# Retention by running state in 36 software-pipelined steps of 128 tokens, in place of full score blocks with the second layer behind

## The chip, the cores and the metric

The kernel runs on one core of one Trainium2 chip. The metric is device microseconds of one execution. Before the change the median of six executions is 512.67 us (512.37 to 516.56).

## The reference

Two layers: multi-head retention (attention with a causal, exponentially decaying mask and no softmax), then a feed-forward layer with a SoLU activation and a layer norm.

```python
# q, k, v: [8 batches, 8 heads, 576 tokens, 64]
scores = (q @ k.T) / sqrt(64)
ret    = scores * where(i >= j, gamma[h] ** (i - j), 0)   # gamma[h] = 1 - 2**(-5-h)
x      = (ret @ v)                                        # as [4608 tokens, 512]
h      = x @ w_in                                         # [4608, 1024]
solu   = h * exp(h - max(h)) / sum(exp(h - max(h)))
ln     = (solu - mean(solu)) / sqrt(var(solu) + 1e-6) * g_ln
out    = ln @ w_out                                       # [4608, 512]
```

## The kernel before

**First layer.** `attention_pair` handles one batch and two heads; it is called 32 times (8 batches, 4 pairs). It loads q, k and v of the pair by twelve DMAs on SP's queue, scales q by gamma^p and k by gamma^-p (p is the token's place in its block of 128) on ScalarE while casting to 16 bits, transposes them on TensorE (L264) and evacuates the transposes (L269 on VectorE, L270 on ScalarE). For each head, all causal score blocks are formed by matmuls with the 64 rows of the head (L283, up to 448 columns at a time), multiplied on VectorE by a table of decays `Gd_sb` that also holds the causal mask (L290), and multiplied by v in two accumulations avA and avB of 288 tokens (L306), whose stationary operand is 64 columns wide. The results go to `xT`, which holds the transposed x of all 4608 tokens (L315, L319).

**Second layer.** The 36 tiles of 128 tokens are handled in groups of four or five. `moe_tile_p1` does h (L131, eight 512-column matmuls), exp with the row sum (L138), the product (L144), mean and variance (L148, L151). After a group's last tile `moe_rstd` takes one square root on ScalarE for the group. `moe_tile_p3` subtracts the mean (L175), transposes on TensorE (L185), evacuates (L188), does the second product (L191, eight 512-column matmuls), scales by 1/std while evacuating (L198) and sends 256 KB out from GpSimd's queue (L201).

**What sets the order.** A scheduler of the framework orders the instructions within each engine by priority and data; the source gives the steps of the batch before after each pair (the loop at L339 to L353). So on TensorE matmuls of the two layers stand between one another. Weights are loaded and cast at the start (L77 to L98), ahead of the first q, k and v on the same queue.

Of the kernel before, what the change touches and what calls it, by code (L numbers as in the profile page):

```python
# [10 lines left out]
F16 = mybir.dt.float16  # L12


def _np_tables():
    H = 8
    P = 128
    gammas = 1.0 - 2.0 ** (-5.0 - np.arange(H, dtype=np.float64))
    p = np.arange(P)
    gq = (gammas[None, :] ** p[:, None]) / 8.0  # L20
    gk = gammas[None, :] ** (-p[:, None])
    rel = p[None, :] - p[:, None]
    M = 576
# [18 lines left out]
def kernel(  # L42
# [14 lines left out]
    P = 128  # L57
    NC = 5
# [3 lines left out]
    gq_np, gk_np, Gd_np, id_np, gammas = _np_tables()  # L62

    const_pool = ctx.enter_context(tc.tile_pool(name="const", bufs=1))
    big_pool = ctx.enter_context(tc.tile_pool(name="big", bufs=1))

    ident = const_pool.tile([P, P], F16)
    gq_sb = const_pool.tile([P, H], FP)
    gk_sb = const_pool.tile([P, H], FP)
    Gd_sb = const_pool.tile([P, H, 576], FP)  # L70
    nc.sync.dma_start(out=ident, in_=nc.inline_tensor(id_np, name="ident").ap())
    nc.sync.dma_start(out=gq_sb, in_=nc.inline_tensor(gq_np, name="gq").ap())
    nc.sync.dma_start(out=gk_sb, in_=nc.inline_tensor(gk_np, name="gk").ap())
# [46 lines left out]
    def moe_tile_p1(t, gi):  # L120
# [26 lines left out]
        for half in range(2):  # L147
# [240 lines left out]
```

## Time and profile before

| | before |
|---|---|
| median of six executions | 512.67 us |
| the profiled execution | 512.37 us |
| its span, first to last instruction | 510.6 us |
| TensorE (PE) busy | 419.2 us, 82% |
| VectorE (DVE) busy | 336.5 us, 66% |
| ScalarE (ACT) busy | 256.9 us, 50% |
| GpSimd (POOL) busy | 19.8 us, 4% |
| mean granted clock of TensorE | 0.877 |
| moved by DMA | 44.8 MB |

The busy share of an engine counts the time in which at least one of its instructions is under way, so a matmul at the lower of the two clocks counts twice as long as at the higher, and a busy TensorE need not be one that does much. "Pitch" below is the time from the start of one matmul to the start of the next. Where a row of the timeline merges n instructions, the pitch is the row's length less one single duration, divided by n - 1.

### The profile page before, as it was taken

Reading aid. Unit: us, or ns where it says so; the run is one execution under the profiler, and the core shown is the slowest. Engines: PE = TensorE matmul, PEld = TensorE weight load, DVE = VectorE, ACT = ScalarE, POOL = GpSimd, SP = SyncE. Lnnn points to the kernel's source line nnn. Section 1 sums busy time; section 2 is a strip of 40 time slices with the busy share of each in tenths; the row PEclk is TensorE's granted clock in tenths of the full one; section 3 lists DMA queues with packets and bytes.
Section 4 is the critical chain, followed back from the end, with each engine's and each line's share of the span. In section 5 each row is a group of like instructions: output and inputs, shape, how many; then the busy total and the mean of one; then the engine's idle time right before and its main releaser. Section 6 shows DMA issues by size and latency. Waiting matters only on the chain.

```text
span 510.6 us, 6542 instructions
## 1 busy us (share of the span) xinstructions
PE 419.2 (82%) x2080; PEld 184.1 (36%) x2080; DVE 336.5 (66%) x953; ACT 256.9 (50%) x597; POOL 19.8 (4%) x40
## 2 busy tenths in 40 slices
PE   0088998989979898889969898889969899789774
PEld 0033443334523443344423444333423444244341
DVE  0256667684788658684588658784687758784850
ACT  1343446445854558154844569144844468043642
POOL 0000000000000100000000010000000000000001
PEclk9999999559978899599978899598987899699979
DMA  7855531426450345214440345204440241000002
GB/s 294 276 121 127 117 89 29 92 66 152 127 112 2 89 127 119 48 35 113 119 98 1 86 113 126 59 24 112 123 104 1 68 116 37 1 22 34 29 22 83
DMA packets 122835, 44.79 MB, mean 88 GB/s; under 512 B 118832, under 2 KB 118832, under 8 KB 122672
## 3 DMA queue, kind: packets, MB, share of 16 engines
q1 hardware_dynamic: 119920, 34.94, 28.2%
q0 software_dynamic: 2880, 9.44, 4.9%
q8 instruction: 16, 0.26, 0.2%
q14 instruction: 19, 0.16, 0.1%
HBM read 34.91 MB, written 9.44 MB: 87 GB/s over the span
## 4 chain that ended last, share of the span: by engine, by line
PE 64%; DVE 19%; ACT 9%; DMA 4%; issue 3%; SPq 1%; POOL 0%; POOLq 0%; ACTq 0%; DVEq 0%
PE ops L191 15%; PE qk L283 15%; PE avB L306 11%; PE hps L131 7%; PE avA L306 6%; DVE stats L148 6%; DVE solu_g L144 6%; DMA gln_sb<-in_moe_g_ln_dram 4%; PE lntp L185 3%; DVE retT L290 3%; PE tk L264 3%; ACT lnT_sb L188 3%; PE tq L264 3%; ACT khT L270 1%; DVE ln_sb L175 1%
## 5 line engine op out<-in xcount | busy, mean ns | idle before, releaser
L290 DVE TENSOR_TENSOR retT<-qk,Gd_sb 128x288 f16<-128x288 f32 (+4 forms) x384 | 150.2, 428 | 81.3 <-PE qk L283 80.4
L283 PE MATMUL qk<-qhT,khT 64*128 64x288 f16 (+4 forms) x384 | 113.0, 326 | 28.6 <-DVE solu_g L144 12.1
L191 PE MATMUL ops<-w2p_sb,lnT_sb 128*128 128x512 f16 x288 | 88.3, 430 | 7.5 <-ACT lnT_sb L188 5.7
L306 PE MATMUL avB<-retT,v 128*64 128x288 f16 (+2 forms) x320 | 93.5, 320 | 0.0
L131 PE MATMUL hps<-w_in_sb,xT 128*128 128x512 f16 x288 | 84.2, 426 | 7.3 <-DVE solu_g L144 7.3
L306 PEld LDWEIGHTS <-v 128*64 128x64 f16 (+1 forms) x512 | 51.5, 122 | 76.4 <-issue 55.5
L138 ACT ACTIVATE e_sb<-hps 128x512 f32<-128x512 f32 x72 | 42.8, 596 | 49.8 <-PE hps L131 34.7
L283 PEld LDWEIGHTS <-khT 64*128 64x128 f16 (+1 forms) x384 | 34.3, 101 | 78.1 <-issue 54.1
L306 PE MATMUL avA<-retT,v 128*64 128x288 f16 (+2 forms) x192 | 54.6, 288 | 0.1
L144 DVE TENSOR_TENSOR solu_g<-hps,e_sb 128x512 f32<-128x512 f32 x72 | 48.7, 683 | 8.9 <-ACT e_sb L138 8.8
L188 ACT COPY lnT_sb<-lntp 128x1024 f16<-128x1024 f16 x36 | 36.0, 1013 | 25.2 <-PE lntp L185 24.8
L198 ACT ACTIVATE out_sb<-ops,rstd_g 128x512 f32<-128x512 f32 x36 | 24.6, 684 | 47.6 <-PE ops L191 29.6
L148 DVE BATCH_NORM_STATS2 stats<-solu_g 128x6 f32<-128x512 f32 x72 | 46.2, 679 | 0.1
L131 PEld LDWEIGHTS <-xT 128*128 128x128 f16 x288 | 28.3, 104 | 45.9 <-issue 22.8
L264 PE MATMUL tq<-ident,q 128*128 128x128 f16 (+1 forms) x160 | 21.8, 234 | 27.5 <-ACT q L238 27.2
L191 PEld LDWEIGHTS <-lnT_sb 128*128 128x128 f16 x288 | 27.5, 106 | 45.8 <-issue 18.4
L315 ACT CAST xT<-avA 64x288 f16<-64x288 f32 x32 | 12.5, 391 | 61.7 <-PE avA L306 61.4
L201 POOL DMA_DIRECT2D out_dram<-out_sb x36 | 19.6, 543 | 486.5 <-ACT out_sb L198 468.8
L185 PE MATMUL lntp<-ident,ln_sb 128*128 128x128 f16 x288 | 28.6, 240 | 11.8 <-DVE ln_sb L175 11.8
L175 DVE TENSOR_SCALAR ln_sb<-solu_g,mu_g 128x512 f16<-128x512 f32 x72 | 31.2, 479 | 3.8 <-PE lntp L185 3.6
L246 ACT ACTIVATE k<-k_sb,gk_sb 128x256 f16<-128x256 f32 x64 | 32.2, 503 | 0.0
L238 ACT ACTIVATE q<-q_sb,gq_sb 128x256 f16<-128x256 f32 x64 | 32.1, 502 | 0.0
(32 smaller groups left out, 275.7 us busy)
## 6 DMA issues: line engine op xcount, KB each, us to landing
out_dram<-out_sb POOLq DMA_DIRECT2D x36, 256.0 KB, 2.6
q_sb<-in_q_dram SPq DMA_DIRECT2D x64, 128.0 KB, 2.4
k_sb<-in_k_dram SPq DMA_DIRECT2D x64, 128.0 KB, 2.4
v_sb<-in_v_dram SPq DMA_DIRECT2D x64, 128.0 KB, 2.4
Gd_sb<-Gd SPq DMA_DIRECT2D x1, 2304.0 KB, 9.1
w_in_f<-in_moe_w_in_dram SPq DMA_DIRECT2D x1, 2048.0 KB, 13.7
w_f<-in_moe_w_out_dram SPq DMA_DIRECT2D x1, 2048.0 KB, 19.0
q_sb<-in_q_dram SPq DMA_DIRECT2D x64, 16.0 KB, 2.4
```

The costliest lines, as they stand in the source:

```text
L131: nc.tensor.matmul(out=ps, lhsT=xT[:, dc, tok0 : tok0 + P], rhs=w_in_sb[:, dc, hh], start=(dc == 0), stop=(dc == 3),)
L138: nc.scalar.activation(out=e_sb[:, hh], in_=ps, func=ACT.Exp, accum_out=sums[:, half : half + 1],)
L144: nc.vector.tensor_tensor(out=solu_g[:, gi, hh], in0=ps, in1=e_sb[:, hh], op=ALU.mult)
L148: nc.vector.bn_stats(out=stats[:, half], in_=solu_g[:, gi, half * 512 : (half + 1) * 512])
L175: nc.vector.tensor_scalar(out=ln_sb[:, hh], in0=solu_g[:, gi, hh], scalar1=mu_g[:, gi : gi + 1], scalar2=None, op0=ALU.subtract, op1=ALU.b ...
L185: nc.tensor.transpose(out=tps[:, c], in_=ln_sb[:, c * P : (c + 1) * P], identity=ident)
L188: nc.scalar.copy(out=lnT_sb, in_=tps)
L191: nc.tensor.matmul(out=o_ps, lhsT=lnT_sb[:, c], rhs=w2p_sb[:, c], start=(c == 0), stop=(c == 7),)
L264: nc.tensor.transpose(out=dst_ps[:, c * P : c * P + ncol], in_=src[rows, c, :], identity=ident[rows, rows],)
L283: nc.tensor.matmul(out=ps[0:jsz, 0:pw], lhsT=khT[dd, j0 : j0 + jsz], rhs=qhT[dd, i0:i1], start=True, stop=True,)
L290: nc.vector.tensor_tensor(out=retT[jb][0:jsz, i0:i1], in0=ps[0:jsz, 0:pw], in1=Gd_sb[0:jsz, h, i0 - j0 : i1 - j0], op=ALU.mult,)
L306: nc.tensor.matmul(out=av[:, lo - i0 : i1 - i0], lhsT=v16[0:jsz, jb, dd], rhs=retT[jb][0:jsz, lo:i1], start=(n == 0), stop=(n == len(jbs) ...
```

## The change

The kernel function is written anew; inputs, outputs and the arithmetic of the reference stay.

- **Retention by state.** Only the diagonal 128x128 score block of each chunk is formed. What earlier chunks give is carried in a state per head, the decayed sum of k-transposed times v (64x64), kept in `gt`: `kv_mm` forms a chunk's part, `state` adds it and decays it by gamma^128 (`g128`).
- **Steps.** The work is cut into 36 steps of 128 tokens with all eight heads: four whole chunks of each batch, and one step for the two 64-token remainders of two batches together. Each step goes through both layers. `x` of a step lives in a small tile, not in a buffer of all tokens.
- **Who does what.** Scaling and casting q, k, v, and the decay and cast of the state, go to GpSimd, as do three operations on one element per partition, the last of them the power -1/2 (so there is no square root on ScalarE). Masking and the product with exp are one VectorE instruction of 1024 columns each; so are exp and each evacuation of transposes on ScalarE.
- **Mean.** It is not subtracted from each tile but taken out of the weights once: `prep_mean` forms the column mean of the scaled w_out, `prep_sub` subtracts it.
- **Order.** It is written out by hand (`manual_schedule`). Iteration i has mm1 of step i, transposes, scores and kv of step i+2, retention output of step i+1, and the second product of step i-3. All PSUM pools have one buffer. In an iteration TensorE runs `mm1` and `mm2` (eight matmuls of 512 columns each), `qk_tp` and `ln_tp` (eight transposes each), `av` (16 matmuls of 128 columns), `scores` (8 of 128) and `kv_mm` (8 of 64); ScalarE runs `ln_ev`, `exp_`, `qk_ev`, `x_ev`, `o_ev`; the three instructions at the end of `stats` and the last two of `state` are GpSimd's.
- **DMA.** One load of q, k or v per step has all eight heads of 128 tokens (256 KB); outputs go on SP's queue; the weights w_in come on ScalarE's queue, and w_out on SP's behind the loads of steps 0 to 2. The 2304 KB table of decays is gone; two masks of 128x128 take its place.

```diff
-    for b in range(B):
...
-        for hp in range(4):
-            attention_pair(b, hp)
-            target = (nsteps * (hp + 1) + 3) // 4
-            while done < target:
-                pending[done]()
...
+    for b in range(0, B, 2):
+        steps += [(b, c) for c in range(4)] + [(b + 1, c) for c in range(4)] + [(b, 4)]
...
+    load(0)
+    for c in range(4):
+        nc.scalar.dma_start(out=w_in_f[:, c], in_=w_in_v[:, c])
+    load(1)
+    load(2)
+    nc.sync.dma_start(out=gln, in_=moe_g_ln.rearrange("(c p) -> p c", p=P))
+    for c in range(0, 8, 4):
+        nc.sync.dma_start(out=w2_f[:, c : c + 4], in_=w2_v[:, c : c + 4])
...
+    def scale(i):
+        nc.gpsimd.tensor_tensor(out=q16, in0=d["qr"], in1=gq_of(c), op=ALU.mult)
+        nc.gpsimd.tensor_tensor(out=k16, in0=d["kr"], in1=gk_of(c), op=ALU.mult)
+        nc.gpsimd.tensor_copy(out=v16, in_=d["vr"])
...
+    def scores(i):
+        for hp in range(4):
+            for e in range(2):
+                dd = slice(e * 64, e * 64 + 64)
+                nc.tensor.matmul(
+                    out=s_ps[:, e, hp], lhsT=qkT[dd, 1, hp], rhs=qkT[dd, 0, hp],
...
+    def mask(i):
+        nc.vector.tensor_tensor(
+            out=ret, in0=d["s"].rearrange("p e h j -> p (e h) j"),
+            in1=masks[:, m].unsqueeze(1).to_broadcast([P, 8, P]), op=ALU.mult,
...
+    def kv_mm(i):
+                nc.tensor.matmul(
+                    out=kv[e * 64 : e * 64 + 64, hp], lhsT=d["k16"][:, h],
+                    rhs=d["v16"][:, h], start=True, stop=True,
...
+    def state(i):
+            nc.vector.tensor_tensor(out=t, in0=d["kv"], in1=cur[b]["gt"], op=ALU.add)
+            nc.gpsimd.tensor_tensor(out=gt, in0=t, in1=g128, op=ALU.mult)
+        nc.gpsimd.tensor_copy(out=s16, in_=gt)
...
+    def av(i):
+                    if c < 4:
+                        mm(e, out=av_ps[dd, hp], lhsT=cur[b][c][dd, hp], rhs=qkT[dd, 0, hp])
...
+                mm(e, out=av_ps[dd, hp], lhsT=d["v16"][:, 2 * hp + e], rhs=d["ret"][:, e * 4 + hp])
...
+    def exp_(i):
+        nc.scalar.activation(out=e_sb, in_=d["h"], func=ACT.Exp, accum_out=se)
...
+    def solu(i):
+        nc.vector.tensor_tensor(out=s16, in0=d["h"], in1=d["e"], op=ALU.mult)
...
+    def stats(i):
+            nc.vector.bn_stats(out=bs[:, half], in_=d["solu"][:, half * 512 : half * 512 + 512])
+        nc.vector.bn_aggr(out=mv, in_=bs)
+        nc.gpsimd.tensor_scalar(
+            out=w, in0=d["se"], scalar1=d["se"], scalar2=1e-6, op0=ALU.mult, op1=ALU.mult
+        )
+        nc.gpsimd.tensor_tensor(out=w2, in0=w, in1=mv[:, 1:2], op=ALU.add)
+        nc.gpsimd.tensor_tensor(out=rs, in0=w2, in1=mhalf, op=ALU.pow)
...
+        LAG = 3
+        for i in range(NS + LAG):
+            if ok(i + 4):
+                load(i + 4)
+            if ok(i - 1):
+                ln_ev(i - 1)
+            if ok(i):
+                mm1(i)
+                exp_(i)
+            if ok(i + 2):
+                qk_tp(i + 2)
+            if ok(i + 1):
+                av(i + 1)
+            if ok(i):
+                solu(i)
+            if ok(i + 2):
+                qk_ev(i + 2)
+            if ok(i + 1):
+                x_ev(i + 1)
+            if ok(i + 3):
+                scale(i + 3)
+            if i == 1:
+                prep_mean()
+            if ok(i - LAG):
+                mm2(i - LAG)
+                o_ev(i - LAG)
+            if ok(i + 2):
+                scores(i + 2)
+                kv_mm(i + 2)
+            if ok(i):
+                stats(i)
+            if ok(i + 2):
+                mask(i + 2)
+                state(i + 2)
+            if ok(i):
+                ln_tp(i)
...
```

On TensorE before, in the second batch, matmuls of three shapes of the array stand between one another: `qk` are score blocks (64 rows), `av` the products with v (64 columns), `lntp` the transposes of the second layer (the whole array).

```order
L185 LDWEIGHTS ln_sb
L185 MATMUL lntp<-ident,ln_sb 128x128
L283 LDWEIGHTS khT
L283 MATMUL qk_512_1139<-qhT,khT 64x64
L306 LDWEIGHTS v_1092
L306 MATMUL avA<-retT_1126,v_1092 64x160
L306 LDWEIGHTS v_1092
L306 MATMUL avB<-retT_1126,v_1092 64x288
L185 LDWEIGHTS ln_sb
L185 MATMUL lntp<-ident,ln_sb 128x128
```

On TensorE after the change, in iteration 3, at the seam between the products with v (`av_ps`) and the second product (`o_ps`); on either side stand blocks of eight alike.

```order
L230 LDWEIGHTS v_409
L230 MATMUL av_ps<-ret,v_409 64x128
L317 LDWEIGHTS lnT
L317 MATMUL o_ps<-w2c_101,lnT 128x512
L317 LDWEIGHTS lnT
L317 MATMUL o_ps<-w2c_101,lnT 128x512
```

What moved: the shape changes from one matmul to the next before, and only at the seams of seven blocks in an iteration now.

On GpSimd before, the only instructions after the start are the 36 output DMAs. After the change one iteration stands there like this: scaling of step i+3, the three one-element operations of step i, the state of step i+2.

```order
L144 TENSOR_TENSOR q_407<-qr,small 128x512
L145 TENSOR_TENSOR k_408<-kr,small 128x512
L146 CAST v_409<-vr 128x512
L291 TENSOR_SCALAR w<-se 128x1
L294 TENSOR_TENSOR w_446<-w,mv 128x1
L295 TENSOR_TENSOR rs<-w_446,small 128x1
L217 TENSOR_TENSOR gt<-tt,small 128x256
L219 CAST s_457<-gt 128x256
```

What moved: eight instructions a step that ScalarE and VectorE did in other forms, or that were not there, queue on GpSimd, with the wait for VectorE's variance (`mv`) and state (`tt`) in front of the next step's scaling.

On ScalarE before, between two pairs of heads of the first batch:

```order
L270 COPY khT<-tk 128x576
L238 ACTIVATE q_366<-q_sb,gq_sb 128x4x64
L242 ACTIVATE q_366<-q_sb,gq_sb 64x64
L315 CAST xT<-avA 64x288
L315 CAST xT<-avB 64x288
L238 ACTIVATE q_366<-q_sb,gq_sb 128x4x64
L242 ACTIVATE q_366<-q_sb,gq_sb 64x64
L246 ACTIVATE k_367<-k_sb,gk_sb 128x4x64
L250 ACTIVATE k_367<-k_sb,gk_sb 64x64
```

and after the change, one iteration:

```order
L310 COPY lnT<-tln 128x1024
L272 ACTIVATE e_sb,se<-h_ps 128x1024
L162 COPY qkT<-tqk 128x1024
L253 CAST xT<-av_ps 128x512
L325 ACTIVATE o_sb<-o_ps,rs 128x512
```

What moved: the eight scalings of a pair left ScalarE, and five instructions of 512 or 1024 columns remain for a step.

## Rows read from the trace of the kernel before

**Rows 1.** The page: busy time by engine; granted clock in 40 slices.

```profile
PE 419.2 (82%) x2080; PEld 184.1 (36%) x2080; DVE 336.5 (66%) x953; ACT 256.9 (50%) x597; POOL 19.8 (4%) x40
PEclk9999999559978899599978899598987899699979
```

**Rows 2.** The page: the chain that ended last, by engine.

```profile
PE 64%; DVE 19%; ACT 9%; DMA 4%; issue 3%; SPq 1%; POOL 0%; POOLq 0%; ACTq 0%; DVEq 0%
```

**Rows 3.** Windows: length, busy us (instructions) of PE, PEld, DVE, ACT, POOL; PEclk; DMA.

```profile
174.00:204.60 30.60, 27.88 (x165) 13.22 (x163) 20.77 (x57) 23.19 (x59) 2.16 (x4) 1.00 0.47 122
204.60:218.20 13.60, 12.29 (x44) 4.69 (x43) 9.37 (x26) 2.17 (x7) 0.00 (x0) 0.50 0.20 44
```

**Rows 4.** Timeline of TensorE: start us, length us, then instruction and count.

```profile
77.81 5.10 PE L131 MATMUL hps<-w_in_sb,xT 128*128 128x512 f16 x14
112.75 3.40 PE L191 MATMUL ops<-w2p_sb,lnT_sb 128*128 128x512 f16 x8 [0.25 <-ACT lnT_sb L188]
175.00 1.89 PE L191 MATMUL ops<-w2p_sb,lnT_sb 128*128 128x512 f16 x8
232.22 0.62 PE L185 MATMUL lntp<-ident,ln_sb 128*128 128x128 f16 x8
```

**Rows 5.** Timeline of TensorE at clock 1.00, single matmuls of changing shape.

```profile
180.03 0.20 PE L306 MATMUL avA<-retT,v 128*64 128x32 f16 x1
180.08 0.29 PE L306 MATMUL avB<-retT,v 128*64 128x288 f16 x1
...
180.95 0.21 PE L306 MATMUL avB<-retT,v 64*64 64x64 f16 x1
181.09 0.36 PE L283 MATMUL qk<-qhT,khT 64*128 64x448 f16 x1
181.38 0.39 PE L191 MATMUL ops<-w2p_sb,lnT_sb 128*128 128x512 f16 x1
181.71 0.31 PE L283 MATMUL qk<-qhT,khT 64*128 64x320 f16 x1
```

**Rows 6.** Groups by shape, ScalarE: busy us, mean ns, idle before.

```profile
L188 ACT COPY lnT_sb<-lntp 128x1024 f16<-128x1024 f16 x36 | 36.0, 1013 | 25.2 <-PE lntp L185 24.8
L138 ACT ACTIVATE e_sb<-hps 128x512 f32<-128x512 f32 x72 | 42.8, 596 | 49.8 <-PE hps L131 34.7 <-DVE ln_sb L175 14.7
L138 ACT ACTIVATION_READ_ACCUMULATOR e_sb<-hps 128x1 f32 x72 | 14.3, 199 | 0.0
L198 ACT ACTIVATE out_sb<-ops,rstd_g 128x512 f32<-128x512 f32 x36 | 24.6, 684 | 47.6 <-PE ops L191 29.6 <-issue 16.2 <-ACT q L242 1.5
```

**Rows 7.** Groups by shape, VectorE.

```profile
L144 DVE TENSOR_TENSOR solu_g<-hps,e_sb 128x512 f32<-128x512 f32 x72 | 48.7, 683 | 8.9 <-ACT e_sb L138 8.8
L290 DVE TENSOR_TENSOR retT<-qk,Gd_sb 128x288 f16<-128x288 f32 x128 | 55.9, 453 | 61.3 <-PE qk L283 60.8
L148 DVE BATCH_NORM_STATS2 stats<-solu_g 128x6 f32<-128x512 f32 x72 | 46.2, 679 | 0.1
L151 DVE BATCH_NORM_AGGREGATE mv<-stats 128x2 f32<-128x12 f32 x36 | 7.1, 197 | 0.0
L254 DVE CAST v<-v_sb 128x512 f16<-128x512 f32 x32 | 13.4, 418 | 0.2
L153 DVE TENSOR_TENSOR sums<-sums 128x1 f32<-128x1 f32 x36 | 5.1, 141 | 0.0
```

**Rows 8.** Groups by shape, GpSimd: one of four like it.

```profile
L372 POOL MEMSET const-float32-1.0<- 128x1 f32 x1 | 0.1, 100 | 0.0
```

**Rows 9.** DMA: a queue with packets, MB, share of 16 engines; an issue with us to landing.

```profile
q1 hardware_dynamic: 119920, 34.94, 28.2%
w_f<-in_moe_w_out_dram SPq DMA_DIRECT2D x1, 2048.0 KB, 19.0
```

**Rows 10.** Timeline, start and end of the span.

```profile
26.12 0.61 PE L264 MATMUL tq<-ident,q 128*128 128x128 f16 x4 [26.12 <-ACT q L238]
...
500.34 1.89 PE L191 MATMUL ops<-w2p_sb,lnT_sb 128*128 128x512 f16 x8 [0.83 <-ACT out_sb L198]
...
503.05 1.89 PE L191 MATMUL ops<-w2p_sb,lnT_sb 128*128 128x512 f16 x8 [0.83 <-ACT out_sb L198]
...
505.03 0.69 ACT L198 ACTIVATE out_sb<-ops,rstd_g 128x512 f32<-128x512 f32 x1 [2.02 <-PE ops L191]
```

More of the change, by code (lines that the diff above doesn't have):

```diff
@@ new lines, in qk_tp, with qk_ev @@
+    def qk_tp(i):
+        d = st[i]
+        tp = ps_tp.tile([P, 2, 4, P], F16, tag="tp", name="tqk")
+        for n, src in enumerate((d["q16"], d["k16"])):
+            for hp in range(4):
+                nc.tensor.transpose(
+                    out=tp[:, n, hp], in_=src[:, 2 * hp : 2 * hp + 2, :], identity=ident
+                )
+        d["tp"] = tp
+    def qk_ev(i):
+        d = st[i]
+        qkT = att.tile([P, 2, 4, P], F16, tag="qkT", name="qkT")
+        nc.scalar.copy(out=qkT, in_=d["tp"])
+        d["qkT"] = qkT
@@ L127, in moe_tile_p1, with x_ev, mm1 @@
+    def x_ev(i):
+        d = st[i]
+        xT = att.tile([P, 4, P], F16, tag="xT", name="xT")
+        nc.scalar.copy(out=xT, in_=d["av"])
+        d["xT"] = xT
+    def mm1(i):
+        d = st[i]
+        h_ps = ps_h.tile([P, DFF], FP, tag="h", name="h_ps")
         for half in range(2):
-            hh = slice(half * 512, (half + 1) * 512)
-            ps = psum_qk.tile([P, 512], FP, tag="qk", name=f"hps{half}")
+            hh = slice(half * 512, half * 512 + 512)
             for dc in range(4):
@@ L184, in moe_tile_p3, with ln_tp, ln_ev @@
+    def ln_tp(i):
+        d = st[i]
+        tp = ps_tp.tile([P, 8, P], F16, tag="tp", name="tln")
         for c in range(8):
             nc.tensor.transpose(
[L186 removed]
+                out=tp[:, c], in_=d["solu"][:, c * P : (c + 1) * P], identity=ident
             )
[L188 to L189 removed]
+        d["ltp"] = tp
+    def ln_ev(i):
+        d = st[i]
+        lnT = moe.tile([P, 8, P], F16, tag="lnT", name="lnT", bufs=4)
+        nc.scalar.copy(out=lnT, in_=d["ltp"])
+        d["lnT"] = lnT
@@ new lines, with prep_mean, prep_sub, ok @@
+    wm = {}
+    def prep_mean():
+        mean = ps_o.tile([P, DM], FP, tag="o", name="w_mean")
+        for c in range(8):
+            nc.tensor.matmul(out=mean, lhsT=ones, rhs=w2c16[:, c], start=(c == 0), stop=(c == 7))
+        wm["mean"] = mean
+    def prep_sub(cs):
+        for c in cs:
+            nc.vector.tensor_tensor(
+                out=w2c16[:, c], in0=w2c16[:, c], in1=wm["mean"], op=ALU.subtract
+            )
+    def ok(i):
+        return 0 <= i < NS
+    with tc.manual_schedule():
+        scale(0)
+        qk_tp(0)
+        qk_ev(0)
+        scale(1)
+        scores(0)
+        kv_mm(0)
+        mask(0)
+        state(0)
+        qk_tp(1)
+        qk_ev(1)
+        prep_w_in()
+        av(0)
+        x_ev(0)
+        scores(1)
+        kv_mm(1)
+        mask(1)
+        state(1)
+        scale(2)
+        load(3)
+        LAG = 3
[34 more added lines that the diff above has]
+                ln_tp(i)
+            if i == 0:
+                prep_scale()
+            if i == 1:
+                prep_sub(range(0, 4))
+            if i == 2:
+                prep_sub(range(4, 8))
```

459 lines of the change are left out of this document (183 added, 276 removed).

## The prediction

> **What bounds the kernel now.** I read the chain that ended last first: TensorE holds 64% of it, VectorE 19%, ScalarE 9% [rows 2], and TensorE is busy for 82% of the span [rows 1]. So the question is why TensorE takes so long over what it does. Three answers, from three views.
>
> First, its clock. At a granted 1.00 eight 512-column matmuls take 1.89 us, a pitch of (1.89 - 0.39) / 7 = 0.214 us; at 0.50 they take 3.40 us, a pitch of (3.40 - 0.39) / 7 = 0.43 [rows 4]. These are the levels of 2.4 and 1.2 GHz. The windows show a stretch at each [rows 3]. The page's clock row starts with nines [rows 1], but at 77.8 us fourteen such matmuls take 5.10 us, a pitch of (5.10 - 0.39) / 13 = 0.36, between the two: the rise falls inside. I take all before it, some 50 us of work, to be at the lower level too, and distrust the nines. The fall at 204.6 us follows work in which TensorE waited for VectorE; in the low stretch it is busy 12.29 of 13.60 us but issues 44 matmuls, one in 0.31 us, against one in 0.185 in the stretch before [rows 3].
>
> Second, changes of shape. At 1.00 a 64-column score block is followed after 0.14 us by 448 columns of another shape, those after 0.29 by a 512-column one, that after 0.33 by 320 columns of a third [rows 5]. At 2.4 GHz the columns alone take 0.027, 0.187 and 0.213 us. Each change costs about 0.11 us. Where the shape stays, 32 columns are followed after 0.05 us [rows 5]. Before, the two layers' matmuls alternate, so hundreds of matmuls pay this.
>
> Third, waits: VectorE's mask instructions and ScalarE's exp sit between dependent matmuls; and the first matmul starts at 26.12 us [rows 10], behind the weights and the table of decays.
>
> **The change part by part.** I price one iteration per engine, at 1.00, then ask whether the order lets the dearest engine run without waits.
>
> *TensorE.* Sixteen 512-column matmuls at 0.215: 3.44 us. Sixteen transposes at (0.62 - 0.22) / 7 = 0.057 [rows 4]: 0.91. The 24 small ones of 128 columns (8 scores, 16 retention) have no row; I take the transposes' 0.057, as they stream as many columns: 1.37. Eight kv matmuls of 64 columns: between 0.027 (columns alone) and 0.057, I take 0.05 from the 32-column row [rows 5]: 0.42. Six changes of shape at 0.11: 0.66. Sum 6.80 us. Bounds: the 32 small ones alternate between two halves of the array, which no row shows. If the halves overlap, they cost half, 5.9 in all; if each of the 29 alternations costs the 0.11 of a change, 3.2 more, 10.0.
>
> *ScalarE.* Two evacuations of 1024 at 1.013, exp of 1024 at about 1.02 (512 columns take 0.596, and 512 more at the slope from 0.596 to the 1.013 of a 1024-column copy add 0.42) plus 0.20 for the sum, output 0.68, x at most the same 0.68 [rows 6]: 4.6 us.
>
> *VectorE.* 288 columns of a product take 0.453 and 512 take 0.683, so 1.03 ns a column; 1024 take 1.21. Two of those, two bn_stats at 0.68, 0.20, and the state's 256 columns at 0.42 [rows 7]: 4.4 us.
>
> *GpSimd.* Only memsets of one element, 0.10 us, show it computing [rows 8]. From below I price its eight instructions as VectorE does the like: two products of 512 (0.68 each), a cast (0.42), a product of 256 (0.42), a cast of 256 (0.3), three of one element (0.14) [rows 7]: 2.9 us. Below that is excluded by nothing, but gains nothing. From above, a second pass over each second operand, priced as a cast (0.42, 0.42 and 0.3), adds 1.1: 4.1. I take 4, with a doubtful upper end: VectorE's rows are those of another engine. The point at which it decides is 6.8 / 2.9, 2.3 times VectorE's price.
>
> The Trainium skill speaks against this move: GPSIMD Engine Reference, section 4.1, says not to use GpSimd for elementwise work, about twice as slow as VectorE for two inputs, and section 3.1 gives 1.96. By that the eight would take up to 5.7 us, an estimate from that page, still under TensorE's 6.8; no run here shows it.
>
> *Does TensorE wait?* With 0 at the start of mm1(i): it ends at 1.7, transposes at 2.2, retention at 3.3, mm2 at 5.1, scores and kv at 6.2, ln_tp at 6.8. ScalarE: ln_ev(i-1) to 1.2, exp when mm1 has drained at 1.9, to 3.1, qk_ev to 4.1, x_ev to 4.8. So qkT is there at 4.1 for scores that start at 5.2, xT at 4.8 for mm1(i+1) at 6.8. VectorE: solu from 3.1 to 4.3, which frees h for 6.8 and feeds ln_tp at 6.3; stats to 5.9, mask from 5.9 to 7.1, state to 7.5, which frees scores and kv for 12.0. The transposes' single bank is freed at 1.2 for 1.7 and at 4.1 for 6.3. GpSimd waits for the variance at 5.9 and the state's sum at 7.5, then decays and casts it to 8.3 and scales step i+4 until some 10.5; the transposes that need it start at 6.8 + 6.8 + 1.7 = 15.3. Nothing waits; the least slack is 0.5 us, ln_ev ahead of qk_tp. What is queued behind GpSimd's waits, scaling, has 4.8 us of slack. So the iteration is TensorE's 6.8.
>
> *Clock.* TensorE then streams without gaps. Fourteen h matmuls in a row brought it up, and it stayed at 1.00 over 30.6 us in which TensorE was busy 27.9 [rows 3, 4]. I take 1.00 from iteration 2 on.
>
> *DMA.* 119,920 packets took 28.2% of the span on 16 engines for 34.94 MB [rows 9]: full use would be 34.94 / (0.282 x 510.6 us), 243 GB/s, so a step's 0.79 MB takes 3.2 us, hidden under 6.8, and loads are four steps ahead. Output DMA on SP waits for o_ev(i-3) near 6.0; behind it stands load(i+5), due 10 us later. The table of decays saves 2.36 MB at the start, but three steps of loads (2.36 MB) stand before w_out.
>
> **The sum.** *Start.* Step 0's loads and w_in, 2.9 MB, at 243 GB/s with 2 us of latency land at some 11 to 13 us, step 1's at 15. Scaling, transposes, evacuation, scores, mask, a second round for step 1, and casts of w_in take it to mm1(0) at about 20. Iterations 0 and 1 at 1.2 GHz, with w_out landing at about 24 to 28 (before: 19.0 us after its issue [rows 9]), its scaling (3 us) and the mean: 8 us each. Iteration 2 starts at 36. *Body.* Iterations 2 to 35: 34 x 6.8 = 231. Eight first chunks have no state matmuls (-0.57 each), four remainder steps no kv (-0.5), iteration 2 no mm2 (-1.7), the last two no attention ahead (-4.3): -12, with 1 back for the remainders' doubled state matmuls: 220. *End.* Three mm2 through one bank: before shows that pattern as 503.05 - 500.34 = 2.71 us each, and 510.6 - 505.7 = 4.9 us from the last evacuation to the end [rows 10]: 13. Span 36 + 220 + 13 = 269; with the 1.8 us around the span of the profiled execution (512.4 against 510.6), **271 us**. That execution is 0.3 us below the median, which changes nothing.
>
> **The rivals.**
> - *The halves overlap.* TensorE: Matmul & The Clock Gate of the Trainium skill, Part 3, states that matmuls on different tiles of the array run at once; no row here has two of them side by side. Here the small matmuls alternate halves, so 32 of them save half of their 1.79 us: 0.9 x 36 = 32 us less, **239 us**. For it: scores go to two banks, kv, retention to two partition halves. Against: 0.05 us is the shortest pitch seen [rows 5], and weights must be loaded for each.
> - *Each alternation costs a change of shape.* 3.2 x 36 = 115 us more: **386 us**. For it: no row shows alternation within a shape. Against: rows 5 show the price at changes of shape alone.
> - *GpSimd becomes the bound.* At 3 times VectorE's price, 8.7 us a step, 1.9 x 36 = 68 more: **340 us**. It decides above 2.3. For it: no computing row; the eight wait in order on VectorE twice.
> - *The clock stays low.* TensorE's streamed 6.14 us double, the changes stay: 12.9 us, 6.1 x 36 = 220 more: **491 us**. Against: a gapless engine is what raised it [rows 4].
> - *Slower.* GpSimd at 4.7 times VectorE's price takes 13.6 us a step, 6.8 x 36 = 245 more, **516 us**; above that, slower than before. One mechanism, the same engine, at a price far from the row.
> - *The change does not do what it says*: single PSUM banks make TensorE wait each iteration. The tightest loop is mm1, exp, solu, 1.9 + 1.2 + 1.2 = 4.3 us, so a miss of 1 us in one handover gives at most 0.5 us of wait: **289 us**.
>
> **How the numbers follow.** Forecast with small waits (255 to 300): 0.60. Overlap: 0.12. GpSimd bound below 3 times (300 to 345): 0.14. Alternation cost: 0.06. Low clock: 0.02; GpSimd dearer than 3 times but faster than before: 0.03. Slower: 0.03. The range from 239 to 345 leaves out 0.11 to 0.14. A measurement tells 0.5% from no change; the cases give faster 0.96, same 0.01, slower 0.03.
>
> **What would show it.** Right: TensorE over 90% busy from 40 us on at a clock of 1.00, iterations 6.8 us apart by the starts of `h_ps`, 512-column pitch 0.215; ScalarE and VectorE near 60%. Wrong: `tqk` transposes waiting for `q16` or `k16` (GpSimd bound); a pitch of `s_ps` or `av_ps` near 0.03 (overlap) or 0.17 (alternation); `h_ps` waiting for `xT` or `solu` (handover). The forecast falls if GpSimd's eight take over 6.8 us, or the first `h_ps` comes after 30 us.

## Result and profile after the change

The changed kernel takes 243.88 us (median; 242.84 to 245.55). The kernel before took 513.08 us beside it, so the ratio is 0.4751, 95% interval 0.4737 to 0.4765: faster, as forecast, and inside the range of 239 to 345 us, but 27 us under the forecast of 271. The likeliest case was not the one that came; the rival in which the halves of the array overlap named 239.

The profiled execution took 242.95 us, with a span of 241.2. First the page: busy time by engine, the granted clock in 40 slices, and the chain that ended last, which answer [rows 1] and [rows 2]; then the DMA queue of [rows 9].

```profile
PE 215.3 (89%) x2248; PEld 120.3 (50%) x2248; DVE 157.9 (65%) x227; ACT 157.0 (65%) x223; POOL 157.1 (65%) x276
PEclk9999997999999999999999999999999999999999
...
q1 hardware_dynamic: 119856, 39.86, 73.6%
...
PE 78%; DVE 9%; DMA 6%; ACT 3%; POOL 1%; issue 1%; ACTq 0%; POOLq 0%; DVEq 0%
```

TensorE is now 89% of the span and 78% of the chain; the three other engines stand level at 65%. The clock row keeps its nines, with one dip. Its first slices can't be read: the granted clock is on record from 25.9 us on, and before that the eight `h_ps` of iteration 0, at 20.48 us, take 3.59 us where the later ones take 1.89.

The same span in windows (columns as in [rows 3]): up to the first w_in matmul, iterations 0 and 1, iterations 2 to 35, and the end.

```profile
0.00:20.48 20.48, 4.99 (x56) 3.16 (x57) 6.24 (x7) 5.68 (x6) 6.67 (x12) 1.00 1.03 244
20.48:34.23 13.75, 12.64 (x121) 6.93 (x121) 8.86 (x13) 8.33 (x13) 7.98 (x13) 1.00 1.04 258
34.23:228.93 194.70, 192.02 (x2052) 107.98 (x2050) 141.78 (x205) 139.87 (x200) 141.75 (x251) 0.99 0.75 169
228.93:241.20 12.27, 5.66 (x27) 2.24 (x24) 1.01 (x3) 3.07 (x4) 0.74 (x2) 0.99 0.26 85
```

In the 194.7 us of the body TensorE idles for 2.7. The DMA engines are 75% busy there.

Next, one whole-chunk iteration on TensorE's timeline (start, length, instruction, count), from one `h_ps` to the next; it answers [rows 4] and [rows 5].

```profile
104.97 1.89 PE L262 MATMUL h_ps<-w_in,xT 128*128 128x512 f16 x8
106.69 0.39 PE L154 MATMUL tqk<-ident,q 128*128 128x128 f16 x4
106.92 0.39 PE L154 MATMUL tqk<-ident,k 128*128 128x128 f16 x4
107.23 0.41 PE L230 MATMUL av_ps<-qkT,s 64*64 64x128 f16 x8
107.57 0.41 PE L230 MATMUL av_ps<-ret,v 128*64 128x128 f16 x8
107.92 1.90 PE L317 MATMUL o_ps<-w2c,lnT 128*128 128x512 f16 x8
109.75 0.40 PE L172 MATMUL s_ps<-qkT 64*128 64x128 f16 x8
110.08 0.32 PE L198 MATMUL kv<-v,k 128*64 128x64 f16 x8
110.33 0.62 PE L302 MATMUL tln<-ident,solu 128*128 128x128 f16 x8
110.78 0.59 PE L262 MATMUL h_ps<-w_in,xT 128*128 128x512 f16 x2
```

No row has a wait in brackets: 110.78 - 104.97 = 5.81 us with no gap. Compare the last block of eight transposes, 0.62 us long, with the three blocks of eight small matmuls that stream as many columns: 0.40 and 0.41. A last matmul of 0.22 us taken off, that is a pitch of (0.62 - 0.22) / 7 = 0.057 us against (0.40 - 0.22) / 7 = 0.026. Most of what the iteration takes less than forecast is in those three rows and the one of `kv`.

Last, what the other engines pay (groups as in [rows 6 to 8]).

```profile
L278 DVE TENSOR_TENSOR solu<-h_ps,e_sb 128x1024 f16<-128x1024 f32 x36 | 44.1, 1224 | 55.5 <-ACT e_sb L272 55.5
L272 ACT ACTIVATE e_sb<-h_ps 128x1024 f32<-128x1024 f32 x36 | 36.9, 1024 | 29.1 <-PE h_ps L262 29.1
L144 POOL TENSOR_TENSOR q<-qr,small 128x512 f16<-128x512 f32 x36 | 37.6, 1045 | 8.6 <-DMA qr<-in_q_dram 8.6
L145 POOL TENSOR_TENSOR k<-kr,small 128x512 f16<-128x512 f32 x36 | 37.9, 1052 | 1.3 <-DMA kr<-in_k_dram 1.1
L146 POOL CAST v<-vr 128x512 f16<-128x512 f32 x36 | 22.6, 629 | 6.4 <-DMA vr<-in_v_dram 5.2
L294 POOL TENSOR_TENSOR w<-w,mv 128x1 f32<-128x1 f32 x36 | 6.9, 191 | 29.4 <-DVE mv L287 28.3
L217 POOL TENSOR_TENSOR gt<-tt,small 128x256 f32<-128x256 f32 x24 | 14.7, 614 | 13.8 <-DVE tt L216 13.8
L295 POOL TENSOR_TENSOR rs<-w,small 128x1 f32<-128x1 f32 x36 | 19.8, 551 | 2.8
```

ScalarE's and VectorE's long waits end at each other and at TensorE's `h_ps`: they follow TensorE, and their idle time costs nothing.

**Where the 270 us went.** This is an account counted from the matmul records of the two traces. Before: columns streamed take 302 us (175 at 2.4 GHz, 127 at 1.2, with all before the rise near 82 us taken as low), 866 changes of shape at about 0.1 us make 87, and TensorE idles for 510.6 - 419.2 = 91 us. After: 212 us of columns (197 and 15), 52 of them in pairs side by side, which saves 26; 201 changes of shape make 20, idle 241.2 - 215.3 = 26. The three costs that the prediction named thus gave back 127 / 2 - 15 / 2 = 56 us by the clock, 67 by the changes of shape and 65 by the waits; fewer columns give 239 - 205 = 34 at 2.4 GHz, the overlap some 26. Together that is 248 of 269 us; the rest I didn't attribute. These are shares of an account, not each one taken away alone: no run gives the new kernel the lower clock or the full score blocks.

### The profile page after: what moved, and what is told of

It is laid out like the page before. It is cut to its first block, busy times and chain, and to the rows that moved or that the text cites. A ratio compares the mean times of both kernels' runs of the same rounds, so it can differ in the third digit from the quotient of the medians.

```text
span 241.2 us, 5866 instructions
## 1 busy us (share of the span) xinstructions
PE 215.3 (89%) x2248; PEld 120.3 (50%) x2248; DVE 157.9 (65%) x227; ACT 157.0 (65%) x223; POOL 157.1 (65%) x276
## 4 chain that ended last, share of the span: by engine, by line
PE 78%; DVE 9%; DMA 6%; ACT 3%; POOL 1%; issue 1%; ACTq 0%; POOLq 0%; DVEq 0%
PE o_ps L317 26%; PE h_ps L262 24%; PE av_ps L230 8%; PE tln L302 7%; PE tqk L154 6%; PE s_ps L172 4%; DMA kr<-in_k_dram 4%; PE kv L198 3%; DVE bs L286 2%; DVE w2c L365 2%; DVE solu L278 2%; DMA masks<-masks 2%; DVE ret L183 1%; DVE w2c L346 1%; ACT e_sb L272 1%; ACT o_sb L325 1%
## 5 line engine op out<-in xcount | busy, mean ns | idle before, releaser
L278 DVE TENSOR_TENSOR solu<-h_ps,e_sb 128x1024 f16<-128x1024 f32 x36 | 44.1, 1224 | 55.5 <-ACT e_sb L272 55.5
L262 PE MATMUL h_ps<-w_in,xT 128*128 128x512 f16 x288 | 71.1, 392 | 1.4 <-ACT xT L253 1.4
L317 PE MATMUL o_ps<-w2c,lnT 128*128 128x512 f16 x288 | 68.3, 380 | 2.4 <-ACT o_sb L325 1.8
L272 ACT ACTIVATE e_sb<-h_ps 128x1024 f32<-128x1024 f32 x36 | 36.9, 1024 | 29.1 <-PE h_ps L262 29.1
L183 DVE TENSOR_TENSOR ret<-s_ps,masks 128x1024 f16<-128x1024 f32 x36 | 42.2, 1173 | 10.6 <-PE s_ps L172 10.6
L286 DVE BATCH_NORM_STATS2 bs<-solu 128x6 f32<-128x512 f16 x72 | 46.3, 685 | 1.2
L310 ACT COPY lnT<-tln 128x1024 f16<-128x1024 f16 x36 | 36.4, 1011 | 12.6 <-PE tln L302 12.4
L144 POOL TENSOR_TENSOR q<-qr,small 128x512 f16<-128x512 f32 x36 | 37.6, 1045 | 8.6 <-DMA qr<-in_q_dram 8.6
L162 ACT COPY qkT<-tqk 128x1024 f16<-128x1024 f16 x36 | 36.2, 1005 | 10.0 <-PE tqk L154 10.0
L145 POOL TENSOR_TENSOR k<-kr,small 128x512 f16<-128x512 f32 x36 | 37.9, 1052 | 1.3 <-DMA kr<-in_k_dram 1.1
```

Of the source, the lines that this page charges most:

```text
L144: nc.gpsimd.tensor_tensor(out=q16, in0=d["qr"], in1=gq_of(c), op=ALU.mult)
L145: nc.gpsimd.tensor_tensor(out=k16, in0=d["kr"], in1=gk_of(c), op=ALU.mult)
L162: nc.scalar.copy(out=qkT, in_=d["tp"])
L183: nc.vector.tensor_tensor(out=ret, in0=d["s"].rearrange("p e h j -> p (e h) j"), in1=masks[:, m].unsqueeze(1).to_broadcast([P, 8, P]), op= ...
L262: nc.tensor.matmul(out=h_ps[:, hh], lhsT=d["xT"][:, dc], rhs=w_in16[:, dc, hh], start=(dc == 0), stop=(dc == 3),)
L272: nc.scalar.activation(out=e_sb, in_=d["h"], func=ACT.Exp, accum_out=se)
```

## The experiments

### Half by half: do the small matmuls overlap, and why?

The first experiment sends the four matmuls of one half of the array and then the four of the other, where the changed kernel alternates.

```
-        for hp in range(4):
-            for e in range(2):
+        for e in range(2):
+            for hp in range(4):
```
(in the scores, the kv matmuls and both retention loops)

> Only the order of the small matmuls inside their blocks changes: in scores, kv and the retention output, all four of one half of the array first, then all four of the other half, where the changed kernel alternates halves. Theory (halves overlap only when neighbours lie on different halves): scores cost 8 x 0.057 + 0.10 = 0.55 us in place of 0.33, kv 0.50 in place of 0.25, the two retention blocks 0.55 in place of 0.34 each, so a step takes 6.7 us in place of 5.82 and the time is about 275 us. Rival (a matmul on half of the array is cheap by itself, whatever its neighbour): 244 us, as the changed kernel.

Measured: 245.21 us (244.02 to 246.06), ratio 0.4785 (0.4756 to 0.4813); the intervals of this and of the changed kernel overlap. An iteration takes 5.86 us, 0.04 more. The score block is 0.41 us long in the timeline of TensorE:

```profile
109.77 0.41 PE L172 MATMUL s_ps<-qkT 64*128 64x128 f16 x8
110.10 0.33 PE L198 MATMUL kv<-v,k 128*64 128x64 f16 x8
```

So the theory on record, that the halves overlap where neighbours in the program alternate, fell. In the built program the four of one half do stand ahead of the four of the other, but the records still start in pairs, 13 ns apart (4 ns in the changed kernel) and 0.056 us from pair to pair. Which record belongs to which half the trace doesn't tell. What this run leaves open is whether the short pitch comes from two halves at all, or is simply the price of small matmuls. The next kernel tells that apart: all eight score matmuls read the same half. (It forms the scores of the even heads twice and leaves out those of the odd ones.)

```
-                    out=s_ps[:, e, hp], lhsT=qkT[dd, 1, hp], rhs=qkT[dd, 0, hp],
+                    out=s_ps[:, e, hp], lhsT=qkT[0:64, 1, hp], rhs=qkT[0:64, 0, hp],
```

> All eight score matmuls of a step use rows 0 to 63 (the odd heads' scores are left out, the even heads' are formed twice), so the count, the sizes and both PSUM banks stay and only the second half of the array is unused. In the run with halves in blocks the time stayed, so the question is open again. Theory (two halves run at once, even when four matmuls of one half stand in front): the scores take 8 x 0.056 + 0.10 = 0.55 us in place of 0.33 in each of 36 steps, 8 us more, about 252 us. Rival (a matmul on 64 rows is cheap by itself): 244 us, pairs still 0.056 apart.

Measured: 251.39 us (251.31 to 251.45), ratio 0.4887 (0.4872 to 0.4901). The timeline of TensorE:

```profile
107.71 0.62 PE L172 MATMUL s_ps<-qkT 64*128 64x128 f16 x8
108.26 0.32 PE L198 MATMUL kv<-v,k 128*64 128x64 f16 x8
```

The same eight matmuls, with the same columns and the same weight loads, take 0.62 us in place of 0.40: the pitch is 0.057, the one that the prediction had put down. The iteration grows from 5.82 to 6.04 us, and 36 x 0.22 = 7.9 us is about what the run is longer by. That the small matmuls cost half because two halves of the array work side by side is thereby shown for the scores; for kv and retention, whose records also start in pairs 4 ns apart, it is the like reading of like rows.

### GpSimd: how far from being the bound?

The products on q are formed twice, then three times, in further buffers; nothing reads the extra ones.

```
-        q16 = nat.tile([P, H, D], F16, tag="q16", name="q16")
-        nc.gpsimd.tensor_tensor(out=q16, in0=d["qr"], in1=gq_of(c), op=ALU.mult)
+        for _ in range(2):                      # range(3), bufs=9 in the second kernel
+            q16 = nat.tile([P, H, D], F16, tag="q16", name="q16", bufs=6)
+            nc.gpsimd.tensor_tensor(out=q16, in0=d["qr"], in1=gq_of(c), op=ALU.mult)
```

> The product that scales q is done twice on GpSimd, into two buffers; results stay. GpSimd then has 4.74 + 1.05 = 5.79 us of work in a whole-chunk step against TensorE's 5.82. Theory (GpSimd is in the shadow of TensorE, with several us of slack for the transposes): 244 to 249 us. Rival (GpSimd's place between VectorE's variance and the next step's transposes is on the path): about 1 us a step more, 280 us.

> The product that scales q is done three times on GpSimd; results stay. GpSimd then has 6.84 us of work in a whole-chunk step, above TensorE's 5.82. Theory (GpSimd becomes the bound once its work exceeds TensorE's): 24 middle chunks at +1.0, 8 first chunks at +0.66, 4 remainders at +0.35, so +31 us, about 275 us, with TensorE waiting for q16 or k16. Rival (other waits add up, GpSimd decides later or sooner): under 255 or over 290 us.

Measured with one more: 245.55 us (243.88 to 245.98), ratio 0.478 (0.4754 to 0.4805), and iterations of 5.82 us as before. With two more: 272.35 us, ratio 0.5308 (0.5275 to 0.5341), and iterations of 6.87 us. The waits of the second (engine, line and what it waited for; us in total, times, longest):

```profile
PE tqk L155 <- POOL k L146: 17.2, 30, 0.9
PE tqk L155 <- POOL q L145: 13.0, 6, 7.6
```

One product of 1.045 us a step is hidden and the second is not: 4.72 + 1.05 = 5.77 lies just under the iteration of 5.82, and 4.72 + 2.09 = 6.81 is the new iteration but for 0.06. The rival of a GpSimd bound was right in its mechanism and in the row that shows it (`tqk` transposes waiting for `k16`), and wrong in the price.

### Changes of shape: put them back, take some away

The first kernel puts the eight retention matmuls of `ret` and `v16` between the eight 512-column matmuls of mm2, one after each, which makes 14 changes of shape more in an iteration; all else stays.

```
+            if i + 4 < NS:
+                av(i + 4, part=c)     # one matmul of the retention block after each of mm2's
...
+            if ok(i - LAG):
+                mm2(i - LAG)
             if ok(i + 1):
...
-                mm2(i - LAG)
                 o_ev(i - LAG)
```

> The eight matmuls of the second product and the eight retention matmuls with v alternate one by one, where the changed kernel runs them in two blocks; the same instructions, the same results. Theory (each change of the array's shape costs about 0.10 us, as before): 14 more changes and the lost overlap of eight small matmuls make 1.4 + 0.2 us a step, 32 steps, so about 295 us. Rival (a change of shape is hidden under the 512 columns that stream): at most 252 us.

Measured: 302.28 us, ratio 0.5891 (0.5837 to 0.5946); iterations of 7.61 us, 1.79 more. On the timeline of TensorE:

```profile
109.27 0.39 PE L322 MATMUL o_ps<-w2c,lnT 128*128 128x512 f16 x1
109.59 0.24 PE L233 MATMUL av_ps<-ret,v 128*64 128x128 f16 x1
109.76 0.39 PE L322 MATMUL o_ps<-w2c,lnT 128*128 128x512 f16 x1
```

A 512-column matmul is followed after 0.32 us, against 0.215 where the shape stays, and a 128-column one after 0.17, against 0.057 for a transpose: 0.11 and 0.12 us for a change, the price that the prediction read from [rows 5]. Part of the 1.79 is also the overlap that retention loses, since its two halves no longer stand together.

The second kernel reorders the blocks so that equal shapes meet: mm2 behind the q and k transposes, both of full height and width, and kv ahead of the scores.

```
-            if ok(i + 1):
-                av(i + 1)
...
-            if ok(i + 1):
-                x_ev(i + 1)
...
                 o_ev(i - LAG)
+            if ok(i + 1):
+                av(i + 1)
+                x_ev(i + 1)
             if ok(i + 2):
-                scores(i + 2)
                 kv_mm(i + 2)
+                scores(i + 2)
```

> Order of an iteration on TensorE: mm1, transposes, mm2, retention, kv, scores, ln transposes. The shape of the array then changes four times in place of six. Theory (a seam costs 0.10 us, nothing else has to wait): 36 x 0.2 = 7 us less, about 237 us. Rival (x and the masks come later, and mm1 or the retention waits for them): 244 us or more.

Measured: 238.87 us (238.74 to 240.97), ratio 0.4653 (0.4632 to 0.4674), clear of the changed kernel's interval and about 2% under it; it is the fastest version here. Its order on TensorE:

```profile
105.26 0.39 PE L154 MATMUL tqk<-ident,q 128*128 128x128 f16 x4
105.49 0.39 PE L154 MATMUL tqk<-ident,k 128*128 128x128 f16 x4
105.71 1.89 PE L317 MATMUL o_ps<-w2c,lnT 128*128 128x512 f16 x8
107.53 0.41 PE L230 MATMUL av_ps<-qkT,s 64*64 64x128 f16 x8
107.87 0.41 PE L230 MATMUL av_ps<-ret,v 128*64 128x128 f16 x8
108.12 0.29 PE L198 MATMUL kv<-v,k 128*64 128x64 f16 x8
108.34 0.40 PE L172 MATMUL s_ps<-qkT 64*128 64x128 f16 x8
```

Behind the transposes the 512-column block now starts without the step of 0.1, and kv starts 0.25 us after the second retention block where `o_ps` started 0.35 after it. The iteration is 5.60 us, 0.22 less: two changes of shape. The time falls by 5.0 us and not by the 7 of the theory, and the rival held in part: where step i+1 is the first chunk of a batch the iteration takes 5.46 us against 5.48, as `h_ps` starts 0.66 us behind `tln` in place of 0.46, its weight load waiting for `xT`.

### The order: written out, or left to the scheduler

```
-    with tc.manual_schedule():
+    if True:
```

> The same instructions, but the order within each engine is left to the framework's scheduler, as in the kernel before. Theory (the gain rests on the order that keeps TensorE without gaps and its shapes in blocks): the scheduler mixes shapes and meets the single PSUM buffers with waits; 7 to 9 us a step, 270 to 350 us. Rival (the gain is in the smaller amount of work; any order of these steps will do): under 252 us.

Measured: 276.82 us, ratio 0.5381 (0.5357 to 0.5405), within the range of the theory on record, but not by its mechanism. The waits of TensorE, and the longest of GpSimd:

```profile
PE tqk L154 <- POOL k L145: 19.9, 20, 3.4
PE tqk L154 <- POOL q L144: 9.5, 6, 5.5
...
POOL w L294 <- DVE mv L287: 67.2, 36, 5.3
```

On TensorE the blocks mostly stay whole (231 changes of shape, against 201), so this is not a loss by changes of shape. The `tqk` transposes wait for GpSimd's products, and GpSimd, which works in order, waits 67 us for the variance, against 28 in the changed kernel; behind the start iterations last from 5.5 to 9.3 us. The order written by hand is worth some 33 us of the gain.

### The old plan without its alternation

This one starts from the kernel before: the steps of the second layer are put off until the first layer is done, instead of standing between its pairs of heads.

```
-            target = (nsteps * (hp + 1) + 3) // 4
-            while done < target:
-                pending[done]()
-                done += 1
+        later += pending
...
-    for st in make_group_steps(tiles):
+    for st in later + make_group_steps(tiles):
```

> The kernel before, with all steps of the second layer put behind the whole first layer; nothing else is changed. It takes away most of the alternation of shapes between the two layers. Theory (shape changes are one part of the loss; the other is that the first layer, paced by the masks on VectorE, leaves TensorE at the lower clock): the first layer runs as in the first batch of the kernel before, where five score matmuls of a pair start at 28.90, 38.79 and 48.63 us, 9.8 us a pair, so 26 + 32 x 9.84 = 341 us, and the 36 tiles behind cost VectorE 4.4 us each, 160 to 200 us: 500 to 545 us, no gain. Rival (the alternation of shapes is the main loss): 480 us or less.

Measured: 520.05 us, ratio 1.0115 (1.0071 to 1.0159) against the kernel before. The two layers on the timeline of TensorE, first from the one, then from the other:

```profile
207.60 0.45 PE L306 MATMUL avA<-retT,v 128*64 128x288 f16 x1
207.84 0.45 PE L306 MATMUL avB<-retT,v 128*64 128x288 f16 x1
...
342.56 6.22 PE L131 MATMUL hps<-w_in_sb,xT 128*128 128x512 f16 x22
```

A retention matmul of 288 columns is followed by another of its shape after 0.24 us, which is what 288 columns take at 1.2 GHz; at 2.4 it would be 0.12. All 32 such pairs, one in each call of `attention_pair`, from 30.5 to 335.4 us, show 0.24: the first layer runs at the lower level for all its 316 us, though TensorE is busy for 290 of them. (The page's clock row shows nines here. Its records begin with the first change of level, at 345 us; until then the row can't be read, as the prediction assumed of [rows 1].) Twenty-two `hps` matmuls in a row bring the clock up, and the second layer then runs at 2.4 GHz for some 170 us, with one fall of 3.4. So pulling the layers apart gives nothing by itself, though it takes away 286 of the 866 changes of shape: what the second layer gains, the first loses, as its matmuls alone don't bring the clock up; what in them keeps it down, no run here shows. In the account above the clock is worth nearly as much as the blocks of one shape (56 us and 67).

### The start: two attempts, both given back

The first load of w_in is put behind the loads of step 1, to bring the first `h_ps` forward.

```
-    for c in range(4):
-        nc.scalar.dma_start(out=w_in_f[:, c], in_=w_in_v[:, c])
     load(1)
+    for c in range(4):
+        nc.sync.dma_start(out=w_in_f[:, c], in_=w_in_v[:, c])
     load(2)
```

> w_in comes on SP's queue behind the loads of steps 0 and 1, not on ScalarE's queue beside them. Theory (the first 20 us are the loads of q, k, v sharing the DMA engines with w_in): q, k and v of step 0 land by 6 us in place of 12, the first h matmul starts near 17 us in place of 20.5, and the time falls by 3 us to 241 us. Rival (w_out and its preparation on VectorE set when the pipeline gets going): the first h matmul is earlier but the time stays at 244 us.

Measured: 244.53 us (244.13 to 245.0), ratio 0.4754 (0.4739 to 0.4769): the same time as the changed kernel. The first `h_ps` came 3 us earlier, and iteration 1 then lasted 12.21 us. TensorE's timeline, and GpSimd's:

```profile
17.53 3.59 PE L262 MATMUL h_ps<-w_in,xT 128*128 128x512 f16 x8 [4.11 <-ACT xT L253]
...
30.06 0.40 PE L154 MATMUL tqk<-ident,q 128*128 128x128 f16 x4 [3.91 <-POOL q L144]
```

```profile
28.96 1.04 POOL L144 TENSOR_TENSOR q<-qr,small 128x512 f16<-128x512 f32 x1 [8.56 <-DMA qr<-in_q_dram]
```

The rival had the time right, by another cause than it named: step 3's q, issued behind w_out, arrives late, and the transposes wait for GpSimd, which waits for the load. So the wait moved to iteration 1, and the clock fell behind it: it is 0.58 from 31.4 to 35.4 us, and the eight `w_mean` matmuls there take 2.99 us, against 1.90 in the changed kernel.

The second attempt starts from the version with fewer changes of shape and brings step 3's load ahead of w_out, whose preparation then comes one iteration later.

```
     load(2)
+    load(3)
...
-        load(3)
...
-            if i == 1:
+            if i == 2:
                 prep_mean()
...
-            if i == 0:
-                prep_scale()
             if i == 1:
-                prep_sub(range(0, 4))
+                prep_scale()
             if i == 2:
-                prep_sub(range(4, 8))
+                prep_sub(range(0, 8))
```

> The order with fewer seams, and the load of step 3 put ahead of w_out on SP's queue, with the scaling of w_out, its mean and the subtraction one iteration later. Theory (the first 30 us are bound by the bytes that must land, and step 3's q stands behind w_out): iterations 0 to 2 lose their wait for q of step 3, some 3 us less, 235 to 237 us. Rival (the second product of step 0 then waits for the eight subtractions on VectorE, and the gain is given back): 239 us or more.

Measured: 241.05 us (240.61 to 241.93), ratio 0.4696 (0.468 to 0.4712): slower than the version that it starts from, not faster. VectorE's timeline:

```profile
40.31 4.86 DVE L366 TENSOR_TENSOR w2c<-w2c,w_mean 128x512 f16<-128x512 f16 x8
```

Iteration 1 fell from 7.47 us to 4.81, but iteration 2 rose from 5.52 to 6.88 and iteration 3 from 8.11 to 11.07: its mm2 waits 4.2 us for eight subtractions that were spread over two iterations before, and then takes 3.25 us in place of 1.89, at a granted clock of 0.55. The theory fell, its rival held. In both, what was taken from one iteration of the start came back in a later one. The DMA engines are full up to 34 us (244 and 258 GB/s in the first two windows above, 8.5 MB), which fits; what the shortest start would be stays open.

## Why the prediction missed by 27 us

**The failed step** is the price of the small matmuls in the sum for TensorE: "I take the transposes' 0.057, as they stream as many columns", with six changes of shape beside it. The forecast put an iteration at 6.80 us; it took 5.82. By blocks, each with the change of shape that closes or opens it, from the starts in the iteration shown above:

| block | forecast, us | measured, us |
|---|---|---|
| `h_ps`, eight | 1.72 | 106.69 - 104.97 = 1.72 |
| `tqk`, eight, and a change | 0.57 | 107.23 - 106.69 = 0.54 |
| retention, state, and a change | 0.57 | 107.57 - 107.23 = 0.34 |
| retention, chunk, and a change | 0.57 | 107.92 - 107.57 = 0.35 |
| `o_ps`, eight, and a change | 1.83 | 109.75 - 107.92 = 1.83 |
| scores, eight, and a change | 0.57 | 110.08 - 109.75 = 0.33 |
| kv, eight, and a change | 0.53 | 110.33 - 110.08 = 0.25 |
| `tln`, eight | 0.46 | 110.78 - 110.33 = 0.45 |

Four rows hold 0.97 of the 0.99 us; every other row is within 0.03. The scores and both retention blocks are cheaper by the overlap. In the kv row somewhat more than half is another thing: a pair starts every 0.032 us there, so 64 columns on one half don't take the 0.05 that was put down for them.

The working had named the overlap as the lower bound, 5.9 a step, and gave it 0.12 against 0.60; the sign on record for it, a pitch of `s_ps` near 0.03, is what the rows show. The reason for that choice was that no row showed two matmuls at once and 0.05 us was the shortest pitch seen. That holds for the rows that were read, not for the trace. The code before has few places for it: between the scores of a pair's two heads, which use the two halves, stands the first head's retention, and all retention goes to one half. But where the transpose of the 64 remaining tokens (rows 0 to 63 of the array) is followed by a score block of the second head (rows 64 to 127), as the built program has it in four places, the score block starts 4 ns later; behind the same transpose a score block of the first head, on the same rows, starts 39 ns later. The trace of before, at 1.00, one place of each kind:

```profile
135.56 0.20 PE L264 MATMUL tq<-ident,q 64*128 64x64 f16 x1
135.57 0.25 PE L283 MATMUL qk<-qhT,khT 64*128 64x192 f16 x1
...
189.41 0.20 PE L264 MATMUL tq<-ident,q 64*128 64x64 f16 x1
189.45 0.30 PE L283 MATMUL qk<-qhT,khT 64*128 64x320 f16 x1
```

In a longer window the timeline merges that transpose with the one before it, and the 4 ns can't be seen. So the overlap could have been read before the change, and 0.12 was too little for it.

TensorE: Matmul & The Clock Gate of the Trainium skill, Part 3, which the prediction cited for this rival, says that matmuls on different tiles of the array run at once with starts about 4 ns apart, and the trace agrees: 4 ns within a pair. The same part says that matmuls keep the order of the program; with one half's four ahead of the other's the block here stayed at 0.41 us, where four of one half and then four of the other, in that order, would have taken at least 0.22 + 6 x 0.057 = 0.56, so on that point the measurement differs.

Three small slips of the working change nothing: the 64-column matmul of [rows 5] is one of retention, not a score block; eight at 0.05 are 0.40 and not 0.42; and four blocks of eight have 28 alternations, not 29.

**The sum.** Start: iteration 2 was forecast at 36 us and began at 34.23; the first `h_ps`, forecast near 20, came at 20.48. Iterations 0 and 1, put at 8 us each at 1.2 GHz, took 6.73 and 7.01, as the clock rose within iteration 0. Body: 220 forecast, 194.7 measured. The cheaper iteration gives 34 x 0.98 = 33 us; 8 came back, because an iteration without state or kv matmuls saves 0.25 to 0.34 us and not 0.5 to 0.57 once these are cheap, and because iterations 2 and 3 had costs that the sum left out. End: 13 forecast, 12.3 measured; three mm2 are 2.8 us apart, as in [rows 10].

**The clock.** It was 1.00 from iteration 2 on, as forecast, with one fall. In windows, iteration 2, and then the first part of iteration 3:

```profile
34.23:40.22 5.99, 4.60 (x60) 2.92 (x57) 5.93 (x10) 3.52 (x5) 5.67 (x10) 0.95 1.23 229
40.22:43.32 3.10, 3.10 (x11) 1.17 (x10) 3.07 (x6) 1.01 (x1) 2.84 (x7) 0.55 1.13 198
```

Iteration 2 has no mm2; TensorE waits for 1.4 of its 6 us, and then the clock falls. The eight `h_ps` of iteration 3 take 3.26 us in place of 1.89. This cost about 1.4 us, once.

**The other engines.** ScalarE was put at 4.6 us a step; by the groups it is 1.02 + 0.19 + 1.01 + 1.01 + 0.60 + 0.69 = 4.5. VectorE was put at 4.4 and is 1.22 + 1.17 + 2 x 0.69 + 0.21 + 0.41 = 4.4. GpSimd was put between 2.9 and 4.1 and taken at 4; its eight take 1.05 + 1.05 + 0.61 + 0.61 + 0.40 + 0.27 + 0.19 + 0.55 = 4.7, 1.6 times VectorE's price. That bound was too low, and it stayed harmless: 4.7 is under 5.8. The estimate from GPSIMD Engine Reference of the Trainium skill, section 3.1, was up to 5.7, at 1.96 times; the 512-column product here is 1.045 / 0.683 = 1.53 times the VectorE product of [rows 7], which reads one operand from PSUM, so here the page's figure, measured at 2048 columns, is too dear. It was a point against the move that the trace answers: slower, but the engine was idle. On VectorE the eight would have made 4.4 + 2.9 = 7.3 us a step, above TensorE's 5.8; that is an estimate from the prediction's prices, and no run shows it.

**No waits.** Right: between 41 and 222 us TensorE waits once, 0.6 us, for w_out's preparation. The slack of 0.5 us at `qk_tp` held even at the shorter iteration.

**DMA.** Undersized: 3.2 us a step counted a step's loads alone. With the output it is 169 GB/s x 5.82 us = 0.98 MB an iteration, at 75% of the engines' time 4.4 us. It stayed hidden, with less room than the text said.

## What to carry to other kernels

When small matmuls use half the array, let the two halves' matmuls share a block of one shape, and count the pair as one: that was worth some 0.8 us of an iteration here, and letting equal shapes meet another 0.2. Before you call an effect unseen, look for it where it could be: search the single records for starts closer together than the columns take, because merged rows hide them. Before moving a load or a preparation earlier, find what stands behind it in its queue: both attempts at the start only moved the wait.

## What was not expected of the hardware

Some of VectorE's instructions and GpSimd's slow each other when both work on SBUF. The casts of w_in on VectorE (1024 columns, groups by shape up to 41 us), first in the changed kernel, where GpSimd scales q and k at the same time, then in the kernel with w_in later, where GpSimd idles:

```profile
L339 DVE CAST w_in<-w_in_f 128x1024 f16<-128x1024 f32 x2 | 3.0, 1515 | 0.0
```

```profile
L339 DVE CAST w_in<-w_in_f 128x1024 f16<-128x1024 f32 x2 | 1.4, 694 | 2.8 <-DMA w_in_f<-in_moe_w_in_dram 2.8
```

The same instruction takes 1515 ns or 694. The scaling of w_out shows the same within one run: in the changed kernel the first, beside GpSimd's product, takes 1.20 us, the second and third, without it, 0.47. GpSimd pays too: beside the casts its product on k takes 1.29 us and its cast of v 1.07, where 1.04 and 0.61 are usual. SBUF — State Buffer of the Trainium skill, "Who interferes with whom", says that such a cast can take a pair of ports that the two engines share, and that one of them then waits for the whole instruction; the trace agrees in that the casts are dear only beside GpSimd. It is not all work on SBUF: bn_stats takes 0.685 us beside GpSimd and took 0.679 before, without it. In the body nothing of this is seen: all solu take 1.21 to 1.23 us and all masks 1.17 to 1.23, with GpSimd at work 73% of the time.

The overlap of the two halves doesn't need neighbours that alternate in the program, against what the theory of the first experiment had on record. In the kernel before it is seen only between matmuls of one shape: 69 neighbours there lie on separate parts of the array but differ in shape, and none starts under 0.14 us after the other. One such pair stands in [rows 5]: the 64 columns at 180.95 and the 448 at 181.09.
